# Gap fills of the exponential tables moved to VectorE, 32-bit fills, and tap weights of 52 columns in an S4 + MLP block

## The chip, the core and the metric

One core of a Trainium2 chip runs the whole kernel. The metric is the device time of one execution in microseconds (us). The five engines that matter have their own instruction streams: TensorE (PE, with its weight loads PEld), VectorE (DVE), ScalarE (ACT), GpSimd (POOL) and SyncE (SP, which issues most DMAs). [...] Against the kernel before, a difference of about 0.3% can be told from none.

## What is computed

```python
def _A_ref(u, A_re, A_im, B_re, B_im, C_re, C_im, log_dt, Dskip):
    dt = jnp.exp(log_dt)[:, None]
    logdA = dt * (A_re + 1j * A_im)
    P = jnp.exp(logdA[:, :, None] * l[None, None, :])        # l = 0 .. 2047, in bf16
    K = jnp.einsum("dn,dnl,dn->dl", Cc, P, dt * Bc).real     # the convolution's taps
    ...                                                      # causal convolution of u with K, + u * Dskip

x = A_u                                                      # 1 x 2048 x 512
h = x + _A_ref(_layernorm(x), ...)                           # 512 channels, 128 states each
h2 = h + _B_ref(_layernorm(h), ...)                          # layernorm, MLP 512 -> 1376 -> 512 with gelu
```

## The kernel before

The powers `P` are not tabulated for every `l`. An index is split in two, and a table of each half is kept per channel: the A half has 20 rows (`NA`), the B half has 33 (`NB`). The product of a row of A with a row of B, summed over the 128 states, is one tap, and TensorE makes it by a matrix product whose contraction runs over the states.

**Tables.** `EA` and `EB` hold the real parts, `IA` and `IB` the imaginary parts, in four chunks of 128 channels (`c` = 0 to 3). All lie in one large SBUF tile named `ar`. Inside a chunk four channels are interleaved: the words of one group of four channels are `4*NP_` (A) or `4*NB` (B) values in a row, a table row being four neighbouring values. `NP_` is 32, so that of 32 rows of an A table only 20 are computed; rows 20 to 31 are the gap, and are filled with zeros by `gap` (L756 in the profile). `EA` is filled in two pieces of two chunks each, `IA` chunk by chunk. Before the change each fill writes bf16 values: 64 runs of 48 values for two chunks of `EA`, 32 runs of 48 for one chunk of `IA`. All five are on GpSimd.

**Start.** GpSimd zeroes a scrap that TensorE uses to clear PSUM (L1459, L1466), then builds the identity matrix `identb` (L752, L753). TensorE spreads `log_dt` over the partitions (L710), ScalarE takes the exponential (L701), TensorE transposes the raw parameters with the identity (L809, L840), and VectorE makes the decay rates: `th[1]` is a product from PSUM (L689) and `th[0]` its negative (a `tensor_scalar` of 512 float32 values, L675). From `th` ScalarE makes 16 exponentials for `EB` (L793), while VectorE goes on with the angles (L694, L677, L689), the size of the coefficients (L847, L852) and the layernorm of the first half of the input (L923, L931). Then ScalarE makes the exponentials of `EA` (L991), and the angles go through DRAM (`S_d`, `HL_d`) to be restacked. Sines of the angles (L1026 for B, L1063 for A) are multiplied into the tables by VectorE (L1036, L1043 and L1068).

**Taps.** `kgen(c)` makes the taps of a chunk: for each group `q` of channels (32 groups, by way of `i`), two column tiles of TensorE (`t` = 0 and 1, at column 0 and 64) each get two matrix products, the real one and the imaginary one, that accumulate into the same PSUM words (L1092). The weights are the A table of a pair of channels, read with a step of four values; the moving operand is the pair's B table, 66 columns, also with a step of four. That is 128 products a chunk, 512 in all. Two channels give 2 x 32 = 64 weight columns: 20 rows and 12 of the gap for the first, the same for the second. Then the result is copied out (`evac`, L616 on ScalarE or L618 on VectorE), and later steps read rows 0 to 19 of each 32.

**Order.** Nothing is scheduled at run time. Every step is an operation with a number in the order in which the code adds it, and the list `ORDER` says in which order they are issued: an entry is twice the operation's number, plus one where the second of its possible engines is taken. Each engine does its own in that order. Entries 54 and 56 are the two fills of `EA`.

Of the kernel before, what the change touches and what calls it, by code (L numbers as in the profile page):

```python
# [11 lines left out]
f32 = mybir.dt.float32  # L12
# [8 lines left out]
CW = 128  # L21
# [4 lines left out]
NA = len(ROWS)  # L26
NP_ = 32
NB = 33
# [247 lines left out]
class VS(V):  # L276
# [13 lines left out]
LAG = {"PE": 0.12, "ACT": 0.20, "DVE": 0.14, "POOL": 0.15, "SP": 0.15}  # L290
OWN = {"PE": 0.0, "ACT": 0.17, "DVE": 0.11, "POOL": 0.1, "SP": 0.0}
ORDER = [
# [35 lines left out]
]  # L328
SLOTS = "0124626046204620462406220246200626224606446426424602606426042060242042604206246240264024604620406240245651620426262341302560134076205472541326036260721452042067563414307136506437056253104574107423"

# [110 lines left out]
def kernel(ctx, tc, A_u, A_A_re, A_A_im, A_B_re, A_B_im, A_C_re, A_C_im, A_log_dt, A_Dskip,  # L441
# [220 lines left out]
    def POOL(cost, f, r=(), w=(), pr=None, hv=0):  # L662
        add("POOL", cost, lambda e: f(), r=r, w=w, pr=pr, hv=hv)
# [88 lines left out]
        gp.memset(identb.ap(), 0.0)  # L752
        gp.affine_select(out=identb.ap(), in_=identb.ap(), pattern=[[-1, P]], compare_op=ALU.not_equal, fill=1.0, base=0, channel_multiplier=1)  # L753
    POOL(0.5, ident_fn, w=[identb], pr=0)
    def gap(tabs, pr):
        POOL(0.8 * len(tabs), lambda: gp.memset(free(tabs[0].lo // 2 + 4 * NA, [[4 * NP_, CW // 4 * len(tabs)], [1, 4 * (NP_ - NA)]]), 0.0), w=[t[NA:NP_] for t in tabs], pr=pr)  # L756
    gap(EA[0:2], 0.05)
    gap(EA[2:4], 0.051)

    def split(x, hl, pr, m=1.0):  # L760
        TS(hl[0], x, m, None, ALU.mult, pr=pr)
# [314 lines left out]
    def kgen(c, pr):  # L1076
# [3 lines left out]
        for grp in KIS:  # L1080
            S.pr = pr + 0.01 * KIS.index(grp)
            p = Ps(n=len(grp))
            first = True
            for nb, (i0, n) in enumerate(grp):
                for lo, hi in ((0, n // 2), (n // 2, n)):
                    def fn(e, p=p, nb=nb, i0=i0, lo=lo, hi=hi):
                        for i in range(lo, hi):
                            for t in range(2):
                                q, f = 16 * t + 2 * ((i0 + i) // 4), (i0 + i) % 4
                                o = pst(p)[64 * t:64 * t + 64, 512 * nb + 2 * NB * i:512 * nb + 2 * NB * i + 2 * NB]  # L1090
                                for ta, tb in ((Ar, Br), (Ai, Bi)):
                                    pe.matmul(o, lhsT=free(ta.lo // 2 + q * 4 * NP_ + f, [[4, 2 * NP_]]), rhs=free(tb.lo // 2 + q * 4 * NB + f, [[4, 2 * NB]]), start=ta is Ar, stop=ta is Ai, tile_position=(0, 64 * t))  # L1092
                    add("PE", 0.064 * (hi - lo), fn, r=[Ar, Br, Ai, Bi], w=[p], new=[p] if first else [])
                    first = False
            i0, n = grp[0]
            N = len(grp)

            def ofn(i0=i0, n=n, N=N):
                return ks().rearrange("p z k i -> p (z k) i")[:, :, i0:i0 + n * N].rearrange("p q (b i) -> p q b i", b=N)

            def ifn(p=p, n=n, N=N):
                return pst(p).rearrange("p (b q) -> p b q", b=N)[:, :, 0:2 * NB * n].rearrange("p b (i q) -> p q b i", q=2 * NB)
            evac(ofn, ifn, 2 * NB * n * N, [p], [kg])
# [397 lines left out]
```

## Time and profile before

| | |
|---|---|
| median of three runs | 233.96 us (233.57 to 234.28) |
| the profiled execution | 234.25 us, of it 232.5 us span of the core |
| granted TensorE clock | 0.989 |
| GpSimd busy | 21.7 us (9%), 28 instructions |
| fills by L756 | 2 of 128x3072 bf16, 3 of 128x1536 bf16 |
| tap products, L1092 | 512, matmul rows 18.5 us and weight load rows 17.3 us in all |

Rows of the profile name a line of the kernel and an engine. A row's duration runs from the start of an instruction to its end, so that it includes any time in which the engine held the instruction and could not go on. Matmul rows overlap: the pace of a sequence is its length over its count, not the mean of a row. "Idle before, releaser" is what the engine waited for. PE share says little, as matmuls are pipelined.

### The profile page before, as it was taken

The numbers are of one execution on the slowest core, as the hardware profiler recorded it, in microseconds if no ns is written. First come the engines' busy times: TensorE is split into PE (matmuls) and PEld (weight loads), VectorE is DVE, ScalarE is ACT, GpSimd is POOL, SyncE is SP. The second block draws the span as 40 slices with busy tenths as digits, with TensorE's granted clock in tenths as the row PEclk, the third lists the DMA queues.
The fourth block names the chain that finished last, engine by engine and source line by source line (L and its number), as shares of the span: only waits on it lengthen the run. The fifth ranks groups of instructions, "written<-read, shape, count | busy, mean of one in ns | idle before, by whom it ended". The sixth has DMA issues, their size and how long they took to land.

```text
span 232.5 us, 6866 instructions
## 1 busy us (share of the span) xinstructions
PE 198.0 (85%) x2981; PEld 114.3 (49%) x2981; DVE 173.0 (74%) x277; ACT 164.3 (71%) x203; POOL 21.7 (9%) x28
## 2 busy tenths in 40 slices
PE   7205579576999999999999878999999999999993
PEld 4002453233775569756567465554444434444452
DVE  2999968999797997688899979989965557113022
ACT  4699999999898997998997687685325404903700
POOL 8200030500020000300000030110000101000000
PEclk9999999999999999999999979999999999999998
DMA  5960173135004956585897991009831052051202
GB/s 157 208 107 17 48 182 93 48 102 181 3 6 93 182 154 162 154 174 146 194 226 161 252 266 40 3 0 226 93 71 42 3 126 68 11 121 40 68 17 73
DMA packets 43159, 25.09 MB, mean 108 GB/s; under 512 B 30197, under 2 KB 40697, under 8 KB 43130
## 3 DMA queue, kind: packets, MB, share of 16 engines
q1 hardware_dynamic: 41576, 22.72, 43.2%
q10 hardware_dynamic: 1554, 1.93, 2.7%
q8 instruction: 23, 0.38, 0.7%
q14 instruction: 6, 0.05, 0.1%
HBM read 14.13 MB, written 5.28 MB: 83 GB/s over the span
## 4 chain that ended last, share of the span: by engine, by line
PE 43%; DVE 30%; ACT 15%; issue 5%; DMA 4%; POOL 1%; ACTq 0%; SPq 0%; DVEq 0%; POOLq 0%
PE ps L1378 13%; PE ps L1362 11%; PE ps L1092 7%; ACT ar L616 6%; ACT ar L1063 5%; DVE ar L1235 5%; DVE ar L689 5%; DVE ar L1210 4%; ACT ar L991 3%; DVE ar L694 3%; PE ps L1245 2%; DVE ar L1323 2%; DVE ar L923 2%; DMA HL_d<-ar 2%; PE ps L946 2%
## 5 line engine op out<-in xcount | busy, mean ns | idle before, releaser
L616 ACT CAST ar<-ps 128x1024 bf16<-128x1024 f32 (+3 forms) x73 | 62.5, 917 | 11.3 <-PE ps L1245 5.7
L1364 ACT ACTIVATE ar<-ps,ar 128x512 bf16<-128x512 f32 (+1 forms) x44 | 27.4, 684 | 34.1 <-PE ps L1362 28.6
L1362 PE MATMUL ps<-ar 128*128 128x512 bf16 (+1 forms) x176 | 40.1, 379 | 0.1
L1378 PE MATMUL ps<-ar 128*128 128x512 bf16 (+3 forms) x187 | 40.2, 367 | 0.0
L1380 DVE TENSOR_TENSOR ar<-ps,ar 128x512 bf16<-128x512 f32 (+1 forms) x17 | 10.6, 654 | 26.7 <-issue 19.7
L1378 PEld LDWEIGHTS <-ar 128*128 128x128 bf16 (+1 forms) x187 | 17.8, 97 | 19.7 <-issue 0.7
L1362 PEld LDWEIGHTS <-ar 128*128 128x128 bf16 (+1 forms) x176 | 17.3, 100 | 20.2 <-issue 0.5
L1235 DVE TENSOR_TENSOR ar<-ar 128x2048 bf16<-128x2048 bf16 x20 | 24.0, 1219 | 1.3 <-PE ps L1245 0.9
L618 DVE CAST ar<-ps 128x1024 bf16<-128x1024 f32 (+4 forms) x18 | 19.5, 1092 | 7.3 <-PE ps L1092 2.6
L1245 PE MATMUL ps<-ar 64*128 64x128 bf16 x672 | 23.2, 225 | 1.9 <-DVE ar L1235 1.7
L1245 PEld LDWEIGHTS <-ar 64*128 64x128 bf16 x672 | 20.4, 99 | 6.9 <-DVE ar L1235 4.1
L689 POOL TENSOR_TENSOR ar<-ar 128x4 f32<-128x4 f32 (+1 forms) x6 | 9.5, 1577 | 140.9 <-DVE ar L694 101.8
L1063 ACT ACTIVATE ar<-ps 128x1024 bf16<-128x1024 int16 x20 | 19.5, 1038 | 1.7 <-PE ps L1061 1.5
L1092 PE MATMUL ps<-ar 128*64 128x66 bf16 x512 | 18.5, 243 | 0.4 <-issue 0.4
L1092 PEld LDWEIGHTS <-ar 128*64 128x64 bf16 x512 | 17.3, 147 | 2.8 <-issue 2.5
L793 ACT ACTIVATE ar<-ar 128x1024 bf16<-128x1024 f32 x16 | 15.6, 1042 | 2.7 <-DVE ar L675 2.7
L946 PE MATMUL ps<-ar 128*32 128x512 bf16 x256 | 16.4, 381 | 1.0 <-DVE ar L931 0.9
L1026 ACT ACTIVATE ar<-ps 128x1024 bf16<-128x1024 int16 x16 | 15.8, 1037 | 0.4 <-PE ps L1018 0.4
L1061 PE MATMUL ps<-ar 128*32 128x256 f16 (+1 forms) x256 | 12.9, 300 | 3.0 <-ACT ar L1063 2.8
L967 PE MATMUL ps<-ar 128*64 128x128 bf16 (+2 forms) x160 | 13.7, 298 | 0.9 <-ACT ar L616 0.9
L694 DVE SCALAR_TENSOR_TENSOR ar<-ar 128x4 f32<-128x4 f32 (+3 forms) x33 | 9.9, 305 | 5.9 <-POOL ar L689 5.4
L1068 DVE TENSOR_TENSOR ar<-ar 128x1024 bf16<-128x1024 bf16 x20 | 13.0, 684 | 0.6 <-ACT ar L1063 0.4
(82 smaller groups left out, 234.4 us busy)
## 6 DMA issues: line engine op xcount, KB each, us to landing
ar<-in_A_u_dram SPq DMA_DIRECT2D x16, 128.0 KB
ar<-in_A_u_dram SPq DMA_DIRECT2D x8, 256.0 KB
out_dram<-ar SPq DMA_DIRECT2D x30, 64.0 KB
ar<-in_B_w_dram SPq DMA_DIRECT2D x3, 344.0 KB
AK_d<-ar SPq DMA_DIRECT2D x2, 512.0 KB
AKc_d<-ar SPq DMA_DIRECT2D x4, 256.0 KB
ar<-tab_TP SPq DMA_DIRECT2D x1, 768.0 KB
ar<-AKc_d SPq DMA_DIRECT2D x3, 256.0 KB
```

Source lines behind the costliest of these rows:

```text
L616: act.copy(out_fn(), in_fn())
L618: dve.tensor_copy(out_fn(), in_fn())
L689: add(eng, tuple(c[q] for q in eng), lambda e: (dve if e == "DVE" else gp).tensor_tensor(oap() if oap else o.ap(), aap() if aap else a.ap( ...
L694: add("DVE", c_dve(n, 1, psum), lambda e: dve.scalar_tensor_tensor(oap() if oap else o.ap(), aap() if aap else a.ap(), f(s), bap() if bap ...
L946: pe.matmul(pst(p)[32 * j:32 * j + 32, 512 * z:512 * z + 512], lhsT=BX.ap()[:, f0 + z, 16 - 16 * c:48 - 16 * c], rhs=src[2 * j + c].ap(), ...
L1063: add("ACT", c_act(1024), lambda e, sc=sc: act.activation(sc.ap().rearrange("p z a b -> p (z a b)").rearrange("p (x a f) -> p a x f", a=4, ...
L1092: pe.matmul(o, lhsT=free(ta.lo // 2 + q * 4 * NP_ + f, [[4, 2 * NP_]]), rhs=free(tb.lo // 2 + q * 4 * NB + f, [[4, 2 * NB]]), start=ta is ...
L1235: dve.tensor_tensor(pq.ap().rearrange("p n d -> p (n d)"), a, b_, ALU.mult)
L1245: pe.matmul(pst(p)[:, 512 * h + 128 * k:512 * h + 128 * k + 128], lhsT=q.ap()[rows, x, :], rhs=TP[w].ap()[rows, f0 // 2 + k, :], start=(n ...
L1362: pe.matmul(pst(p)[:fs], lhsT=w1s[dc].ap()[:, fc * P:fc * P + fs], rhs=ybuf.ap().rearrange("p (t c) k -> p c t k", c=4)[:, dc], start=(dc ...
L1364: add("ACT", c_act(512, 1), lambda e, p=p, fc=fc, fs=fs: act.activation(hT.ap()[:fs, fc, :], pst(p)[:fs], ACT.Gelu_apprx_tanh, bias=b1_sb. ...
L1378: pe.matmul(pst(p)[:, c0:c1], lhsT=hT.ap()[:fs, fc, 128 * t:128 * t + 128], rhs=w2s[fc].ap()[:fs, c0:c1], start=(fc == 0), stop=(fc == NFC ...
```

## The change

The two fills of `EA` go to VectorE, ahead of its first product; the three of `IA` stay with GpSimd. All five write float32 words, half as many as bf16 values before. The tap products take 52 columns of weights (32 + 20): the second channel's 12 gap columns are left off, and PSUM partitions 52 to 63 (and 116 to 127) aren't written any more; nothing reads what they would hold.

```diff
 ORDER = [
-    2, 0, 52, 4, 58, 50, 62, 154, 6, 64, ...
+    2, 0, 52, 4, 58, 54, 56, 50, 62, 154, 6, 64, ...
...
-    def gap(tabs, pr):
-        POOL(0.8 * len(tabs), lambda: gp.memset(free(tabs[0].lo // 2 + 4 * NA, [[4 * NP_, CW // 4 * len(tabs)], [1, 4 * (NP_ - NA)]]), 0.0), w=[t[NA:NP_] for t in tabs], pr=pr)
-    gap(EA[0:2], 0.05)
-    gap(EA[2:4], 0.051)
+    def gap(tabs, pr, eng="POOL"):
+        add(eng, 0.8 * len(tabs), lambda e: (gp if eng == "POOL" else dve).memset(V(ar, tabs[0].lo, f32, (CW // 4 * len(tabs), 2 * NP_)).ap()[:, :, 2 * NA:], 0.0), w=[t[NA:NP_] for t in tabs], pr=pr)
+    gap(EA[0:2], 0, "DVE")
+    gap(EA[2:4], 0, "DVE")
...
-                                o = pst(p)[64 * t:64 * t + 64, 512 * nb + 2 * NB * i:512 * nb + 2 * NB * i + 2 * NB]
+                                o = pst(p)[64 * t:64 * t + 32 + NA, 512 * nb + 2 * NB * i:512 * nb + 2 * NB * i + 2 * NB]
                                 for ta, tb in ((Ar, Br), (Ai, Bi)):
-                                    pe.matmul(o, lhsT=free(ta.lo // 2 + q * 4 * NP_ + f, [[4, 2 * NP_]]), rhs=free(tb.lo // 2 + q * 4 * NB + f, [[4, 2 * NB]]), start=ta is Ar, stop=ta is Ai, tile_position=(0, 64 * t))
+                                    pe.matmul(o, lhsT=free(ta.lo // 2 + q * 4 * NP_ + f, [[4, NP_ + NA]]), rhs=free(tb.lo // 2 + q * 4 * NB + f, [[4, 2 * NB]]), start=ta is Ar, stop=ta is Ai, tile_position=(0, 64 * t))
```

VectorE's stream at its beginning, as a piece of the difference (`ar` is the SBUF tile, `ps` PSUM; L708 writes the row of ones for L710, L788 a small constant):

```order
 L708 MEMSET ar 1x128
 L788 MEMSET ar 128x1
+L756 MEMSET ar 128x64x24 x2
 L689 TENSOR_TENSOR ar<-ps,ar 128x512 [waits PE_49,Activation_49]
 L675 TENSOR_SCALAR ar<-ar 128x512 [waits DVE_49]
```

Two fills of 64 runs of 24 words now stand ahead of L689, the first product, and ahead of its wait for TensorE and ScalarE.

GpSimd's stream at the same place and as far as the first fills of `IA` (L901 is a small constant, L1394 and L1395 set the middle row of the B tables):

```order
 L753 AFFINE_SELECT ar<-ar 128x128 [waits Pool_49]
 L901 MEMSET ar 128x16
-L756 MEMSET ar 128x64x48 x2
 L1394 MEMSET ar 128x32x4 x2
 L689 TENSOR_TENSOR ar<-ar 128x8 [waits DVE_49,Pool_49]
 L1394 MEMSET ar 128x32x4
 L1395 MEMSET ar 128x32x4 [waits DVE_49,Activation_49]
-L756 MEMSET ar 128x32x48
+L756 MEMSET ar 128x32x24
```

The two fills of 64 runs of 48 values are gone from GpSimd, and its small fills L1394 follow right behind L901. The fills of `IA` keep their places with half the values in a run. TensorE, ScalarE and SyncE issue the same instructions in the same order as before, the tap products with 52 weight columns for 64.

70 rows, old and new, of the table ORDER are left out of this document.

## The prediction

> **What bounds the kernel now.** I read the chain of waits first, for the stages that set the end, then in time order for its first 12 us, where the fills are.
>
> ```profile
> PE 43%; DVE 30%; ACT 15%; issue 5%; DMA 4%; POOL 1%; ACTq 0%; SPq 0%; DVEq 0%; POOLq 0%
> PE ps L1378 13%; PE ps L1362 11%; PE ps L1092 7%; ACT ar L616 6%; ACT ar L1063 5%; DVE ar L1235 5%; DVE ar L689 5%; DVE ar L1210 4%; ACT ar L991 3%; DVE ar L694 3%; PE ps L1245 2%; DVE ar L1323 2%; DVE ar L923 2%; DMA HL_d<-ar 2%; PE ps L946 2%
> ```
>
> The bound moves from engine to engine. The fills L756 do not appear in it; the tap products L1092 do, with 7%.
>
> ```profile
> 3.71 0.61 PE ps L809 x4
> 4.42 0.70 DVE ar L689
> 5.15 2.52 DVE ar L675
> 7.67 0.60 DVE ar L694
> ```
>
> From 4.42 us VectorE is the chain. One piece is out of proportion: L675, a `tensor_scalar` of 512 float32 values, for 2.52 us. The views of single lines (shortest, median, longest in ns) and the timeline say why.
>
> ```profile
> L675 DVE TENSOR_SCALAR ar<-ar x6: 420/428/2524, 5.1 to 40.8; 128x512 f16<-128x512 f32 x5, 128x512 f32<-128x512 f32 x1
> L677 DVE TENSOR_SCALAR ar<-ar x4: 420/426/427, 8.3 to 39.6; 128x512 f32<-128x512 f32 x4
> L1394 POOL MEMSET ar<- x4: 199/204/205, 7.0 to 69.5; 128x128 bf16 x4
> 1.84 5.26 POOL L756 MEMSET ar<- 128x3072 bf16 x2
> 7.04 0.35 POOL L1394 MEMSET ar<- 128x128 bf16 x2
> 7.71 2.00 ACT L793 ACTIVATE ar<-ar 128x1024 bf16<-128x1024 f32 x2 [2.70 <-DVE ar L675]
> ```
>
> The same form (L677) takes 0.43 us. Taking that from the end of L675 (5.15 + 2.52 = 7.67) gives 7.24 us; GpSimd's two fills end at 1.84 + 5.26 = 7.10, and the first L1394 at 7.04 + 0.20 = 7.24. So L675 stood until GpSimd paused, 2.52 - 0.43 = **2.1 us**, and ScalarE's L793 stood behind it. L689, from 4.42 to 5.12 in the middle of the same fills, took its usual 0.70: not every VectorE form is stopped, but this one is.
>
> Is there room behind the stall? A table by stage (columns: stretch, then busy us of PE, PEld, DVE, ACT, POOL, then clock, DMA share, GB/s):
>
> ```profile
> 8.00:16.00 8.00, 0.00 (x0) 0.10 (x1) 7.83 (x14) 8.00 (x9) 0.00 (x0) 1.00 0.88 169
> 16.00:26.00 10.00, 3.17 (x37) 1.67 (x40) 9.86 (x18) 10.00 (x13) 0.00 (x0) 1.00 0.07 24
> 26.00:37.00 11.00, 9.09 (x209) 6.43 (x202) 7.76 (x22) 10.98 (x13) 2.11 (x2) 1.00 0.67 164
> ```
>
> From 8 to 26 us VectorE and ScalarE are both full, to 37 us ScalarE still is. Both start behind L675, so both move as a whole.
>
> **The change part by part: the stall.** GpSimd's two fills leave; after the identity (L753, rows below, to 1.85) it has L901 and two L1394 of 0.20 left, and is done by about 2.4 us, long before L675 comes. The stall goes: **-2.1 us** where L675 ends. What is late next? Loads that do not move. The layernorm's first reading (L923) stands at 19.95 us, and would stand at 17.85; PE's first use of the table of identity weights (L865) at 17.55, and would at 15.45:
>
> ```profile
> 13.68 0.10 PEld L865 LDWEIGHTS <-ar 128*32 128x32 f16 x1 [6.87 <-DMA ar<-tab_I]
> 17.55 0.37 PE L865 MATMUL ps<-ar 128*32 128x256 f16 x1 [10.44 <-DVE ar L675]
> 19.95 0.68 DVE L923 BATCH_NORM_STATS2 ar<-ar 128x6 f32<-128x512 bf16 x1
> 14.00:16.00 2.00, 0.00 (x0) 0.00 (x0) 1.97 (x3) 2.00 (x3) 0.00 (x0) 1.00 0.27 40
> ```
>
> That table has landed at 13.68, and DMA falls to 0.27 between 14 and 16 us, so the input is in by then; about 2 us are left over. SP issues the `S_d` and `HL_d` transfers when VectorE has made their contents, so they come 2.1 us earlier too, and the tables behind them in SP's queue with them. I see nothing with a fixed time that eats the gain; I keep 1.9 to 2.2.
>
> **The fills on VectorE.** Two instructions of 64 x 24 = 1536 words, between L788 and L689. No such fill is in the trace; the nearest are VectorE's own small ones.
>
> ```profile
> L788 DVE MEMSET ar<- x1: 59/59/59, 0.9 to 0.9; 128x1 f32 x1
> L1280 DVE MEMSET ar<- x1: 112/112/112, 8.2 to 8.2; 128x64 uint32 x1
> 0.72 0.62 POOL L1459 MEMSET ar<- 1x640 bf16 x1 [0.29 <-POOLq L1485]
> 0.81 0.17 DVE L708 MEMSET ar<- 1x128 bf16 x1 [0.81 <-PEq L1485]
> 0.92 0.06 DVE L788 MEMSET ar<- 128x1 f32 x1
> 1.29 0.20 POOL L752 MEMSET ar<- 128x128 bf16 x1
> 1.56 0.29 POOL L753 TENSOR_SCALAR_AFFINE_SELECT ar<-ar 128x128 bf16<-128x128 bf16 x1
> ```
>
> 63 more words cost 53 ns, 0.84 ns each: 1536 words take 1.35 us, two 2.7 us. From 0.98 they end at 3.7, and L689 cannot start before L809 ends at 3.71 + 0.61 = 4.32. The cover is 4.42 - 0.98 = 3.4 us, so I cost them at **0**. As an upper bound for a word I take L689's own rate, 0.70 us for 512 values, 1.37 ns: 2.1 us each, end 5.2, L689 0.8 late. If the cover goes (a shorter PSUM clearing, say), they cost their 2.7.
>
> [...]
>
> Beside them GpSimd builds the identity (L752, L753, 1.29 to 1.85), which L809 needs at 3.7: a fill that kept GpSimd out of SBUF until 3.7 would make L809 0.6 late (0.20 + 0.29 and hand-over). Before, L708 and L788 ran inside GpSimd's L1459, and L708's 128 values took 0.17, no more per value than L1280's 64 in 0.11, so I take 0.
>
> **The `IA` fills** on GpSimd get shorter or stay (half the values). Nobody waits for L756 by its own view, and GpSimd is 9% busy: 0 either way. Should L1394 or these ever meet a `tensor_scalar`, each costs at most its length.
>
> **52 columns.** Nearly all of L1092 is on the path: its pieces in the chain, of which the first, the two longest and the last are shown, add up to 497 of the 512, one half in each of two stages (to 71 us, and from 83.6 us). What sets their pace?
>
> ```profile
> 59.17 2.37 PE ps L1092 x68
> 68.61 2.41 PE ps L1092 x68
> 87.32 4.21 PE ps L1092 x130
> 94.65 1.15 PE ps L1092 x32
> ...
> 87.16 4.38 PE L1092 MATMUL ps<-ar 128*64 128x66 bf16 x132
> 107.86 0.64 PE L967 MATMUL ps<-ar 128*64 128x128 bf16 x16
> L1092 PE MATMUL ps<-ar 128*64 128x66 bf16 x512 | 18.5, 243 | 0.4 <-issue 0.4
> L967 PE MATMUL ps<-ar 128*64 128x128 bf16 x64 | 2.5, 221 | 0.0
> L1092 PEld LDWEIGHTS <-ar 128*64 128x64 bf16 x512 | 17.3, 147 | 2.8 <-issue 2.5
> L967 PEld LDWEIGHTS <-ar 128*64 128x64 bf16 x160 | 7.0, 110 | 5.0 <-issue 3.3
> L1362 PEld LDWEIGHTS <-ar 128*96 128x96 bf16 x16 | 2.0, 122 | 1.7 <-issue 0.3
> L946 PEld LDWEIGHTS <-ar 128*32 128x32 bf16 x256 | 5.9, 96 | 7.6 <-issue 2.3 <-DVE ar L931 1.2
> ```
>
> The pace is (4.38 - 0.24) / 131 = 31.6 ns for L1092, and (0.64 - 0.22) / 15 = 28.0 ns for L967, which also alternates two column tiles of 64 weight columns, but reads 128 moving columns without a step. L1092's 66 columns take as long a row as L967's 128 (243 for 221), and its weight load of 64 columns is 37 ns longer than L967's. So both of its operands, read with a step of four, seem to come at about half rate: 66 like 132. Were the moving side alone the limit, the pace would be 28.0 x 132 / 128 = 28.9 ns; it is 31.6, so I read the weight load as the limit, by 2.7 ns. A column of weights costs (122 - 96) / 64 = 0.41 ns, at half rate 0.81: 12 fewer save 9.8 ns a load, 4.9 with two tiles side by side, more than the 2.7. Then the moving side limits: 2.7 ns x 497 = **-1.3 us**. Bounds: 0 if the load does not limit; 31.6 x 12 / 64 = 5.9 ns x 512 = 3.0 us if the load is all there is. I stay at 1.3, the one that a row (L967) prices. ScalarE and VectorE have to follow:
>
> ```profile
> 58.50:72.00 13.50, 13.09 (x368) 10.29 (x356) 12.19 (x16) 11.73 (x14) 1.52 (x2) 1.00 0.02 4
> 83.50:97.00 13.50, 13.46 (x360) 11.66 (x360) 9.88 (x24) 11.46 (x15) 2.16 (x2) 1.00 0.49 134
> ```
>
> In both stages PE is full and they have 1.3 to 3.6 us to spare, so 0.65 each fits.
>
> **Sum.** 234.25 (the profiled execution: 232.5 span and 1.75 around it) - 2.1 - 1.3 = 230.85. That execution lay 0.29 above the median of 233.96, so against it: **230.6 us**.
>
> **The rivals.** *Only the stall goes.* The moving 66 columns set L1092's pace and the 31.6 is theirs, with some loss from the step; narrower weights change no pace. For it: matmul rows are stretched (243) just as the loads are. Against: L967's 28.0. 234.25 - 2.1, on the median's scale 231.9.
> [...]
>
> *Only the taps gain.* The wait of L675 reappears: the fills on VectorE end late, or VectorE and GpSimd block each other at 1 to 4 us, or L675 waits for something other than GpSimd. Against: the end at 7.24 to the hundredth. 234.25 - 1.3, so 232.7.
>
> *Neither*: 234.0, no change.
>
> *Slower: the fill pays for each run.* VectorE's fill has 64 runs of 24 words; if each costs a start like L788's 59 ns, a fill takes 1.35 + 64 x 0.059 = 5.1 us, two end at 11.2, L689 is 6.8 late, and the whole chain behind it: 234.25 + 6.8 - 2.1 - 1.3, so 237.4. A fill starts to cost over 1.72 us (half of 3.44), and over 3.4 us both gains are gone. Against: GpSimd's fills have the same 64 runs, and 3072 values in 2.66 us (half of 5.26 and a hand-over) are no dearer per value than 128 in 0.20.
>
> **How the numbers follow.** Both gains 0.60 (its own range 229.2 to 231.5: start 1.9 to 2.2, taps 0.5 to 2.8); only the stall 0.20; only the taps 0.10; neither 0.05; slower 0.05. The predicted time is the first case's, 230.6. The range 229.2 to 232.8 takes in the first three and leaves out the last two and the tails. Faster by over 0.3% (under 233.26; about what a measurement of this kernel can tell) are the first three, 0.90; within 0.3% 0.05; slower 0.05.
>
> **What would show it.** Right: L675 near 5.15 us takes 0.43, L793 starts near 5.6, L756 on VectorE twice about 1.35 us and over before 4.3, HL_d and everything to 48 us 2.1 earlier, L1092 at 28 to 29 ns. Wrong: L689 after 4.5 us (the fills are too long), L675 long again, L923 or L865 with a DMA for releaser (a load is next), L1092 still at 31 to 32 ns, or ScalarE idle no less between 58 and 72 us.

## The result, and the profile after

| | before | after |
|---|---|---|
| median of five runs each | 233.96 us (233.37 to 234.34) | 230.90 us (230.66 to 231.47) |
| the profiled execution | 234.25 us, span 232.5 | 230.71 us, span 228.9 |
| granted TensorE clock in it | 0.989 | 0.997 |
| L675, longest | 2.52 us | 0.43 us |
| pace of L1092 | 31.6 ns | 31.2 ns |

The ratio is 0.9876, with a 95% interval of 0.9851 to 0.9900: faster by 2.3 to 3.5 us.

The page of the changed kernel, its chain by engine and by line:

```profile
PE 53%; ACT 26%; DVE 10%; DMA 4%; issue 4%; POOL 1%; ACTq 0%; SPq 0%; DVEq 0%; POOLq 0%
PE ps L1362 17%; PE ps L1378 17%; ACT ar L616 8%; PE ps L1092 7%; ACT ar L793 7%; ACT ar L1063 5%; ACT ar L991 4%; PE ps L1245 4%; DVE ar L1235 2%; DMA HL_d<-ar 2%; PE ps L946 2%; DMA ar<-AKc_d 2%; DVE ar L971 1%; DVE ar L1068 1%; ACT ar L701 1%
```

VectorE's share fell from 30% to 10% and ScalarE's rose from 15% to 26%. That is a change of route more than of work: between 8 and 26 us both engines are full (VectorE 17.8 of 18 us, ScalarE 18.0), and the chain now goes back over ScalarE's L793 where it went over VectorE's L694 and L689. L1092 keeps its 7%.

The timeline of the start (start, duration, engine, line, what; in brackets the idle time before and its releaser):

```profile
1.25 1.34 DVE L756 MEMSET ar<- 128x1536 f32 x1 [0.27 <-issue]
1.84 0.35 POOL L1394 MEMSET ar<- 128x128 bf16 x2
2.86 1.34 DVE L756 MEMSET ar<- 128x1536 f32 x1 [0.27 <-issue]
4.42 0.69 DVE L689 TENSOR_TENSOR ar<-ps,ar 128x512 f32<-128x512 f32 x1 [0.22 <-ACT ar L701]
5.15 0.43 DVE L675 TENSOR_SCALAR ar<-ar 128x512 f32<-128x512 f32 x1
5.61 2.00 ACT L793 ACTIVATE ar<-ar 128x1024 bf16<-128x1024 f32 x2 [0.60 <-DVE ar L675]
...
15.45 0.37 PE L865 MATMUL ps<-ar 128*32 128x256 f16 x1 [8.69 <-DVE ar L675]
...
17.84 0.68 DVE L923 BATCH_NORM_STATS2 ar<-ar 128x6 f32<-128x512 bf16 x1
```

L675 takes its usual 0.43 us at the same start of 5.15, and L793 starts at 5.61 where it started at 7.71. The loads behind do not eat the gain: L865 and L923 come 2.1 us earlier, at 15.45 and 17.84, and L865 still waits for VectorE, not for a DMA. The fills end at 2.86 + 1.34 = 4.20, 0.22 ahead of L689. But a row of 1.34 reads short: the two starts lie 1.61 us apart, and the 0.27 of "idle" before each belongs to the fill. 1.61 us for 1536 words are 1.05 ns a word.

The groups of the tap products (count, then busy us and mean ns of a row), one long run of them, and the second of their two stages (busy us of PE, PEld, DVE, ACT, POOL, then clock, DMA share, GB/s):

```profile
L1092 PE MATMUL ps<-ar 128*52 128x66 bf16 x512 | 18.3, 242 | 0.4 <-DVE ar L1068 0.4
L1092 PEld LDWEIGHTS <-ar 128*52 128x52 bf16 x512 | 16.8, 128 | 2.7 <-issue 1.8 <-DVE ar L1068 0.6
```

```profile
84.94 4.33 PE L1092 MATMUL ps<-ar 128*52 128x66 bf16 x132
```

```profile
81.00:94.00 13.00, 13.00 (x348) 11.00 (x344) 9.74 (x22) 11.32 (x15) 2.16 (x2) 1.00 0.45 128
```

The weight load became 19 ns shorter (147 to 128), the matmul row 1 ns (243 to 242), and the pace is (4.33 - 0.24) / 131 = 31.2 ns. PE is as full in its stage as before (13.00 of 13.00 us, and 13.46 of 13.50 before). The copies out of PSUM (L616 and L618, 128x924 values in their rows) still read all 128 partitions, those that are no longer written included; only the steps behind them leave these rows out.

**Where the two profiled executions part.** The start of the same instruction in both, from the views of the chain and the timeline:

| instruction | before | after | earlier by |
|---|---|---|---|
| L793, first | 7.71 | 5.61 | 2.10 |
| L1092, first | 59.17 | 57.07 | 2.10 |
| L616, after the last tap products | 96.83 | 94.53 | 2.30 |
| L971, its run of four | 114.96 | 112.27 | 2.69 |
| L1380, the last of VectorE | 228.93 | 225.39 | 3.54 |

So 2.1 us come from the start, 0.2 from the tap stages, 0.4 at L971, which nobody had foreseen, and 0.85 later. The last is put down to TensorE's clock and not to the change. The stretch from 132 to 141 us, before the change and then after it, and the same 64 products in both (they start 2.70 us apart, and what follows them 3.4 to 3.7):

```profile
132.00:141.00 9.00, 5.67 (x106) 4.42 (x100) 7.22 (x16) 7.32 (x11) 1.93 (x1) 0.81 0.99 249
...
135.58 3.41 PE L1245 MATMUL ps<-ar 64*128 64x128 bf16 x64 [1.68 <-DVE ar L1235]
```

```profile
132.00:141.00 9.00, 7.00 (x154) 5.45 (x155) 8.09 (x13) 7.82 (x14) 1.69 (x1) 1.00 0.84 171
...
132.88 1.96 PE L1245 MATMUL ps<-ar 64*128 64x128 bf16 x64 [1.46 <-DVE ar L1235]
```

TensorE was granted 0.81 of its clock there on average in the profiled execution of before (0.50 from 136 to 138 us), and the full clock in that of after. Why such a dip comes is not shown; it comes in some executions of nearly every kernel here. Of the 23 executions of before beside the first experiments, the four at a granted clock of 1.0 took 233.0 to 233.3 us, those at 0.985 to 0.990 took 234.0 to 234.5, about 1 us more. The mean clock alone doesn't tell what a dip costs: the two executions at 0.948 and 0.956 took 233.1 and 233.3.

The two executions of after at 1.0 took 230.7 and 230.9. Without dips the difference is so some 2.1 to 2.7 us; the three terms 2.1, 0.2 and 0.4 add up to 2.7, its upper end.

### The profile page after: what moved, and what is told of

Its sections match the earlier page's. It is cut to its first block, busy times and chain, and to the rows that moved or that the text cites. A ratio compares the mean times of both kernels' runs of the same rounds, so it can differ in the third digit from the quotient of the medians.

```text
span 228.9 us, 6859 instructions
## 1 busy us (share of the span) xinstructions
PE 196.2 (86%) x2974; PEld 113.6 (50%) x2981; DVE 173.5 (76%) x279; ACT 164.4 (72%) x203; POOL 14.6 (6%) x26
## 4 chain that ended last, share of the span: by engine, by line
PE 53%; ACT 26%; DVE 10%; DMA 4%; issue 4%; POOL 1%; ACTq 0%; SPq 0%; DVEq 0%; POOLq 0%
PE ps L1362 17%; PE ps L1378 17%; ACT ar L616 8%; PE ps L1092 7%; ACT ar L793 7%; ACT ar L1063 5%; ACT ar L991 4%; PE ps L1245 4%; DVE ar L1235 2%; DMA HL_d<-ar 2%; PE ps L946 2%; DMA ar<-AKc_d 2%; DVE ar L971 1%; DVE ar L1068 1%; ACT ar L701 1%
## 5 line engine op out<-in xcount | busy, mean ns | idle before, releaser
L616 ACT CAST ar<-ps 128x1024 bf16<-128x1024 f32 (+3 forms) x73 | 62.4, 917 | 10.8 <-PE ps L1245 5.3
L1380 DVE TENSOR_TENSOR ar<-ps,ar 128x512 bf16<-128x512 f32 (+1 forms) x17 | 10.6, 652 | 26.7 <-issue 19.7
L618 DVE CAST ar<-ps 128x1024 bf16<-128x1024 f32 (+4 forms) x18 | 19.5, 1091 | 6.6 <-PE ps L1092 2.5
L1245 PE MATMUL ps<-ar 64*128 64x128 bf16 x672 | 21.5, 216 | 1.9 <-DVE ar L1235 1.5
L1245 PEld LDWEIGHTS <-ar 64*128 64x128 bf16 x672 | 19.1, 94 | 6.5 <-issue 3.2
L1092 PE MATMUL ps<-ar 128*52 128x66 bf16 x512 | 18.3, 242 | 0.4 <-DVE ar L1068 0.4
L689 POOL TENSOR_TENSOR ar<-ar 128x4 f32<-128x4 f32 (+1 forms) x6 | 9.5, 1577 | 143.3 <-DVE ar L694 104.6
L1092 PEld LDWEIGHTS <-ar 128*52 128x52 bf16 x512 | 16.8, 128 | 2.7 <-issue 1.8
L793 ACT ACTIVATE ar<-ar 128x1024 bf16<-128x1024 f32 x16 | 15.6, 1044 | 0.6 <-DVE ar L675 0.6
L694 DVE SCALAR_TENSOR_TENSOR ar<-ar 128x4 f32<-128x4 f32 (+3 forms) x33 | 9.9, 305 | 6.4 <-POOL ar L689 5.4
L967 PE MATMUL ps<-ar 128*64 128x128 bf16 (+2 forms) x160 | 13.6, 298 | 0.9 <-ACT ar L616 0.9
(83 smaller groups left out, 229.0 us busy)
```

What stands on the lines that cost most here:

```text
L616: act.copy(out_fn(), in_fn())
L618: dve.tensor_copy(out_fn(), in_fn())
L793: add("ACT", c_act(1024) + 0.03, lambda e, e0=e0: act.activation(free(EB0 // 2 + 4 * (16 - e0), [[8 * e0, 2], [4 * NB, NCH * CW // 4], [1, ...
L1092: pe.matmul(o, lhsT=free(ta.lo // 2 + q * 4 * NP_ + f, [[4, NP_ + NA]]), rhs=free(tb.lo // 2 + q * 4 * NB + f, [[4, 2 * NB]]), start=ta is ...
L1245: pe.matmul(pst(p)[:, 512 * h + 128 * k:512 * h + 128 * k + 128], lhsT=q.ap()[rows, x, :], rhs=TP[w].ap()[rows, f0 // 2 + k, :], start=(n ...
```

## The experiments

The questions: which part of the change removes the stall, what sets the pace of the taps, how near the fills are to the path, and what happened at L971. Medians of before beside them lay between 233.68 and 233.95 us. "Before" or "after" behind a label is the kernel that the edit starts from.

**The fills alone** (e1, after).

```diff
-o = pst(p)[64 * t:64 * t + 32 + NA, ...]
+o = pst(p)[64 * t:64 * t + 64, ...]
-lhsT=free(ta.lo // 2 + q * 4 * NP_ + f, [[4, NP_ + NA]])
+lhsT=free(ta.lo // 2 + q * 4 * NP_ + f, [[4, 2 * NP_]])
```

> The change without its narrow weights (64 columns again). Theory: the fills give the 2.1 us of L675's stall, and the 52 columns next to nothing, since the changed kernel's tap products still go at 31.2 ns (31.6 before). Then this is within 0.3 us of the changed kernel: 231.0 to 231.3, L1092 back at 31.6 ns. Rival (the 52 columns give the 1.3 us forecast for them): 232.2.

231.55 us (230.75 to 231.84), ratio 0.9899 [0.9878, 0.9920]. The start is that of after row by row, and the long run of tap products takes 0.02 us more than with 52 columns:

```profile
85.11 4.35 PE L1092 MATMUL ps<-ar 128*64 128x66 bf16 x132
```

(4.35 - 0.24) / 131 = 31.4 ns. L971's run of four starts at 112.49, 0.22 later than in after (112.27): that is all that the taps brought. The median is 0.25 above what was expected. Most of the 0.65 us between it and that of after is likely dips: five of these six executions had one, and the sixth, at a clock of 1.0, took 230.75.

**The narrow taps alone** (e2, before, with the two lines of e1 the other way round).

> The 52 columns alone, fills as before. Theory: 0.1 to 0.3 us faster than before, 233.7; L675 keeps 2.52 us, L1092 at 31.2 ns, its weight load rows shorter (128 ns for 147), its matmul rows unchanged. Rival (the weight load sets the pace somewhere): 1 us or more, 232.7 or less.

233.73 us (232.79 to 234.37), ratio 0.9997 [0.9980, 1.0014], over twelve executions. The stall stands as before, and the pace is (4.33 - 0.24) / 131 = 31.2:

```profile
5.15 2.52 DVE L675 TENSOR_SCALAR ar<-ar 128x512 f32<-128x512 f32 x1
...
87.06 4.33 PE L1092 MATMUL ps<-ar 128*52 128x66 bf16 x132
```

The weight load shrank here too, from 147 to 129 ns a row, and the interval takes in no change. The weight load did not set the pace; the forecast's 1.3 us is not there.

**32-bit fills on GpSimd** (e3, before). Fills not moved, 64 columns.

```diff
-gp.memset(free(tabs[0].lo // 2 + 4 * NA, [[4 * NP_, CW // 4 * len(tabs)], [1, 4 * (NP_ - NA)]]), 0.0)
+gp.memset(V(ar, tabs[0].lo, f32, (CW // 4 * len(tabs), 2 * NP_)).ap()[:, :, 2 * NA:], 0.0)
```

> The kernel before with 32-bit fills and nothing else: the fills stay on GpSimd, at their old place, with 64 columns. Theory (what counts is that GpSimd is done when L675 comes at 5.15 us, not who fills): the GpSimd fills halve to about 1.4 us each and end by 4.7 us, L675 takes 0.43 us, the time is that of the fills-only run, 231.0 to 231.3. Rival (GpSimd must not fill at all beside VectorE's work, or L675 waits for something else): L675 stays over 1 us, 232.5 to 234.

```profile
1.84 2.70 POOL L756 MEMSET ar<- 128x1536 f32 x2
4.42 0.69 DVE L689 TENSOR_TENSOR ar<-ps,ar 128x512 f32<-128x512 f32 x1 [3.44 <-ACT ar L701]
4.48 0.35 POOL L1394 MEMSET ar<- 128x128 bf16 x2
5.15 0.43 DVE L675 TENSOR_SCALAR ar<-ar 128x512 f32<-128x512 f32 x1
```

GpSimd's fill, too, costs by values and not by bytes here: half the values in as many bytes take 2.70 us for 5.26. Its fills end at 4.54, before L675 comes, and the stall is gone without a fill being moved. The time, 231.97 us (231.31 to 232.10), ratio 0.9913 [0.9892, 0.9934], is 0.7 above what was expected: 0.4 of it is L971 (below), the rest dips in four of six executions (the two at a clock of 1.0 took 231.3).

**16-bit fills on VectorE** (e4, after). The pieces of EA are filled as bf16 values, with ones. The IA fills on GpSimd are bf16 again too (1.38 us each in before, 0.74 in after; by the views of L756 nobody waits for them there).

```diff
-.memset(V(ar, tabs[0].lo, f32, (CW // 4 * len(tabs), 2 * NP_)).ap()[:, :, 2 * NA:], 0.0)
+.memset(free(tabs[0].lo // 2 + 4 * NA, [[4 * NP_, CW // 4 * len(tabs)], [1, 4 * (NP_ - NA)]]), 0.0 if eng == "POOL" else 1.0)
```

> The changed kernel with the two fills on VectorE in bf16, 3072 values each for 1536 words (filled with ones, which nothing reads). The fill's true price is told by what it delays. Theory (one value takes 1.04 ns, as the 1.61 us from one fill's start to the next's shows, and the row of 1.34 us leaves 0.27 out): 3.2 us each, the second ends at 7.4, L689 3.0 us late, 233.9. Rival (the rows are right, 0.84 ns a value): the second ends near 6.2, L689 1.8 late, 232.7. Rival (a start is paid for each of the 64 runs): later than 10 us, 237 or more.

```profile
1.57 2.62 DVE L756 MEMSET ar<- 128x3072 bf16 x1 [0.59 <-issue]
4.78 2.62 DVE L756 MEMSET ar<- 128x3072 bf16 x1 [0.59 <-PE ps L809]
7.33 0.62 DVE L689 TENSOR_TENSOR ar<-ps,ar 128x512 f32<-128x512 f32 x1
7.98 0.43 DVE L675 TENSOR_SCALAR ar<-ar 128x512 f32<-128x512 f32 x1
```

From start to start 4.78 - 1.57 = 3.21 us for 3072 values, 1.04 ns each, the same as for a word of 32 bits. L689 comes 2.9 us later than in after, and the median is 233.91 us (233.58 to 234.75), ratio 1.0009 [0.9993, 1.0024]: to move the fills without halving them would have brought nothing.

**The operands of the taps without their step** (e5 and e6, after; one execution each). Other values are multiplied, so the taps are others.

```diff
-rhs=free(tb.lo // 2 + q * 4 * NB + f, [[4, 2 * NB]])
+rhs=free(tb.lo // 2 + q * 4 * NB + f, [[1, 2 * NB]])
```

> The changed kernel; the moving operand of the tap products is 66 neighbouring values, not every fourth (the taps come out as other numbers, the work is the same). Theory (the moving operand, read at half rate because of its step, sets the 31.2 ns): the matmul rows fall from 242 by some 28 ns to about 215, and the pace below 27 ns. Rival (two products in a row on one column tile, or the weight load, set it): pace still 30 to 32 ns.

```profile
L1092 PE MATMUL ps<-ar 128*52 128x66 bf16 x512 | 15.2, 216 | 0.4 <-DVE ar L1068 0.4
L1092 PEld LDWEIGHTS <-ar 128*52 128x52 bf16 x512 | 14.4, 145 | 2.8 <-issue 1.8 <-DVE ar L1068 0.6
...
83.16 3.48 PE L1092 MATMUL ps<-ar 128*52 128x66 bf16 x132
```

(3.48 - 0.22) / 131 = 24.9 ns, 6.3 below after; 228.69 us. L971 comes 2.85 us earlier than in after. The 24.9 need not be the moving operand's own pace: L967 passes 128 columns without a step in 28.0 ns, by which 66 would take some 14 (an estimate: 28.0 x 66 / 128). So something else may limit here, and the step itself may cost more than 6.3.

```diff
-lhsT=free(ta.lo // 2 + q * 4 * NP_ + f, [[4, NP_ + NA]])
+lhsT=free(ta.lo // 2 + q * 4 * NP_ + f, [[1, NP_ + NA]])
```

> The changed kernel; the weights of the tap products are 52 neighbouring values, not every fourth (other taps, same work). Theory (the moving operand sets the pace): the weight load rows fall from 128 to about 105 ns, the pace stays at 31 ns. Rival (the weight load still sets it): pace 28 ns or less.

```profile
L1092 PEld LDWEIGHTS <-ar 128*52 128x52 bf16 x512 | 16.3, 121 | 2.5 <-issue 1.6 <-ACT ar L616 0.4 <-DVE ar L1068 0.2
...
84.39 4.25 PE L1092 MATMUL ps<-ar 128*52 128x66 bf16 x132
```

(4.25 - 0.24) / 131 = 30.6 ns, 0.6 below after, and 230.63 us. The weight load rows fell to 121 ns only, not to the 105 that was expected. Taking the step from the moving operand brings 6.3 ns a product, taking it from the weights a tenth of this: the moving 66 columns, read with their step, set the pace.

**The two tiles in turn** (e7, after; e8 the same with 64 columns, one execution).

```diff
-for t in range(2):
-    ...
-    for ta, tb in ((Ar, Br), (Ai, Bi)):
+for ta, tb in ((Ar, Br), (Ai, Bi)):
+    for t in range(2):
```

> The changed kernel with the two column tiles taking turns: real product of tile 0, real of tile 1, imaginary of 0, imaginary of 1, for 0, 0, 1, 1. The 28.9 ns of the forecast came from L967, which takes turns. Theory (two products in a row on one tile leave a gap, since the second one's operands wait for the first): pace 28 to 29.5 ns, tap stages 0.5 us shorter each, 229.7 to 230.4. Rival (each product's own moving read, 66 columns at half rate, sets the pace in any order): pace 31 ns, 230.9.

> As the run before, with 64 weight columns again. Theory: if taking turns brings the pace under 30 ns, the weight load is the next limit and 64 columns cost something again, a pace 1 to 2.5 ns above that of 52 columns. Rival: the same pace as with 52 columns, so the width plays no part in either order.

A run of 132 takes 4.33 us in e7, as in after, and in e8 4.35, as in e1. e7 took 231.46 us (230.67 to 231.62), ratio 0.9890 [0.9867, 0.9913], e8 230.90. The order of the tiles brings nothing with either width, as the rivals said.

**A short clearing of PSUM, and the fills late** (e9, e10 and e11, after). e9 makes only one of the four products L1466 that clear PSUM with zeros; e10 also returns the fills of EA to GpSimd, as words, at about 40 us; e11 returns them with all four products.

```diff
-zero(zs[:4])
+zero(zs[:1])
```

> The changed kernel with one of the four PSUM-clearing matmuls (L1466) at the start, so that L710, the exponential and L809 can come up to 1.1 us earlier; the fills stay on VectorE ahead of L689. It takes away the cover of the fills. Theory (a fill holds VectorE 1.61 us, the second to 4.2 us, whatever its row of 1.34 says): L689 starts near 4.2, not 3.3; 230.7. Rival (the fills are done by 3.6, as row lengths from 0.98 would say): L689 near 3.6, 230.1. Rival (the parameters come too late, or TensorE is slower without the clearing): L689 at 4.4, 230.9 or more.

```profile
2.86 1.34 DVE L756 MEMSET ar<- 128x1536 f32 x1 [0.27 <-issue]
3.14 1.16 PE L809 MATMUL ps<-ar 128*128 128x128 bf16 x8 [0.19 <-DMA ar<-in_A_A_re_dram]
4.13 0.61 DVE L689 TENSOR_TENSOR ar<-ps,ar 128x512 f32<-128x512 f32 x1
4.78 0.43 DVE L675 TENSOR_SCALAR ar<-ar 128x512 f32<-128x512 f32 x1
```

230.42 us (230.24 to 231.32), ratio 0.9853 [0.9831, 0.9874]. TensorE's L809 comes 0.5 us earlier and now waits for a load; L675 comes 0.37 earlier, and L689 stands behind the second fill without a gap: now the fills come last.

```diff
-2, 0, 52, 4, 58, 54, 56, 50, 62, ...
+2, 0, 52, 4, 58, 50, 62, ...
...
-348, 280, 492, ...
+348, 280, 54, 56, 492, ...
...
-gap(EA[0:2], 0, "DVE")
-gap(EA[2:4], 0, "DVE")
+gap(EA[0:2], 0)
+gap(EA[2:4], 0)
```

> The same short clearing, with the two EA fills as 32-bit words on GpSimd right behind the IA fills, at 40 us and over. Nothing is then left on VectorE ahead of L689. Theory: L689 near 3.3 us, L675 takes 0.43 there, and all of the 1.1 us is kept: 229.8, faster than the changed kernel by 1 us. Rival (the next limit at the start, ScalarE's table load or the loads, comes within 0.3 us): 230.6. Rival (fills at 40 us stand in the way of VectorE's or TensorE's work there): slower than 230.9.

```profile
2.94 1.21 PE L809 MATMUL ps<-ar 128*128 128x128 bf16 x8 [0.29 <-DMA ar<-in_A_A_re_dram]
3.72 0.69 DVE L689 TENSOR_TENSOR ar<-ps,ar 128x512 f32<-128x512 f32 x1 [2.74 <-PE ps L809]
4.45 0.43 DVE L675 TENSOR_SCALAR ar<-ar 128x512 f32<-128x512 f32 x1
```

Without the fills L689 comes at 3.72, 0.70 earlier than in after and 4.13 - 3.72 = 0.4 earlier than in e9. About half of this is not the fills: L809 waits for its parameters in both traces, and they came 0.2 us later in e9 (3.14 for 2.94). In e10 as in after L689 starts 0.78 us behind the start of L809, which in e9 would be 3.92; so the fills cost some 0.2 us there, 0.4 at most, and not their 2.7. What L675 gains over e9, 0.33 us, is given back at L971 (below): 230.48 us (230.40 to 231.02), ratio 0.9865 [0.9845, 0.9885], no better than e9. The 229.8 of the theory is missed by 0.7: L689 comes at 3.72 and not near 3.3, and 0.37 goes at L971.

> The changed kernel with full clearing and only the EA fills moved, to GpSimd at 40 us, as 32-bit words. Theory (on VectorE they stand inside its 3.4 us of waiting and cost nothing, at 40 us GpSimd's fills stop nobody): the time of the changed kernel, 230.7 to 231.2, L689 at 4.42. Rival (the fills on VectorE cost something that L689's start does not show): 0.5 us faster.

With the full clearing and the fills away L689 and L675 start at 4.43 and 5.15, as in after: the fills on VectorE cost nothing there. But the time is 231.96 us (231.83 to 232.09), ratio 0.9922 [0.9904, 0.9939], 1 us above after. That missed what was expected by 0.8, and no row of the start answers for it. 0.4 stands at L971, and its six executions all had a dip (clock 0.993 or less); that the dips are the rest is not shown.

**Two small instructions more on VectorE** (e12, e3 with L788 three times instead of once). In before and e2, e3, e10 and e11 L971 starts 0.36 to 0.37 us later behind L967 than in after and e1, e4 to e9. The second set has two VectorE instructions more ahead of it, the fills; so the theory is that L971's place in VectorE's stream counts, and the rival that GpSimd's fills do.

```diff
-lambda e: dve.memset(tiny.ap(), 1e-36)
+lambda e: [dve.memset(tiny.ap(), 1e-36) for _ in range(3)]
```

> The kernel before with 32-bit fills on GpSimd (the run e3), and the one-value fill L788 on VectorE three times for once. Its two more instructions do no work, but VectorE's stream is as long again ahead of L689 as in the changed kernel. It is about the 0.37 us by which a VectorE instruction (L971, near 112 us) starts later after its wait in every kernel whose EA fills are on GpSimd, and in none where VectorE has them. Theory (it is the place in VectorE's instruction stream at which that wait falls, and two instructions more move it): in the profile L971 starts about 0.07 us after its wait's row, as in the changed kernel, and the time is 0.3 to 0.4 us under that of e3: 231.6. Rival (GpSimd's fills themselves do it): 0.42 us after the wait's row, 232.0.

231.39 us (231.03 to 231.84), ratio 0.9900 [0.9878, 0.9922], beside e3's 231.97; at a clock of 1.0 it is 231.0 beside 231.3. The same run of four in before, after, e3, e11 and e12, in this order:

```profile
114.96 2.48 DVE L971 TENSOR_TENSOR ar<-ps,ar 128x512 bf16<-128x512 f32 x4 [0.76 <-PE ps L967]
```

```profile
112.27 2.48 DVE L971 TENSOR_TENSOR ar<-ps,ar 128x512 bf16<-128x512 f32 x4 [0.39 <-PE ps L967]
```

```profile
112.81 2.48 DVE L971 TENSOR_TENSOR ar<-ps,ar 128x512 bf16<-128x512 f32 x4 [0.75 <-PE ps L967]
```

```profile
112.70 2.48 DVE L971 TENSOR_TENSOR ar<-ps,ar 128x512 bf16<-128x512 f32 x4 [0.75 <-PE ps L967]
```

```profile
112.58 2.48 DVE L971 TENSOR_TENSOR ar<-ps,ar 128x512 bf16<-128x512 f32 x4 [0.39 <-PE ps L967]
```

With a constant written twice more, 110 us earlier, the wait falls from 0.75 to 0.39, GpSimd's fills being those of e3. In all fourteen kernels, by one trace of each, it is 0.75 or 0.76 without the two instructions and 0.39 with them. The place in the stream counts; why it does no run here shows.

## Why the prediction was near, and where it was wrong

Forecast 230.6 us, measured 230.9, in the range and with the sign. But the sum was 2.1 + 1.3, and what was found is 2.1 + 0.2 + 0.4 and a share of dips that fell on one side. That the total came so near is partly luck: 1.1 us too much for the taps was made up by 0.4 at L971 and by the dips.

**The stall: right, to the hundredth.** L675 at 5.15 for 0.43, L793 at 5.61, L865 at 15.45 and L923 at 17.84 stand where they were put, and everything to the tap stages is 2.1 us earlier. The cause holds as well: e3 leaves the fills on GpSimd and only lets them end at 4.54, ahead of L675, and the stall is gone. No semaphore explains the stall: L675's only wait, in the stream shown with the change, is for VectorE itself (DVE_49). What held it instead no run shows. What is shown is that L675 stood for 2.1 us while GpSimd filled, and takes 0.43 us when GpSimd's fills are over (e3) or not there (after); L689, a product of 512 values with one operand from PSUM, had its 0.69 us in the middle of the same fills.

**The fills at nothing: right, with less cover than the rows gave.** The row has 1.34 us where 1.35 was put, and the end at 4.20 was asked to be before 4.3. But a fill really takes 1.61 us, of which its row leaves out 0.27. From 0.98 two of them end at 4.20, where the second row ends too, and not at the 3.7 of the prediction; before L689 at 4.42 that leaves 0.22 us of cover and not 4.42 - 3.7 = 0.7. e4 shows how narrow it was: at 3.21 us a fill the whole gain is gone. The rival that each run of 24 words costs a start is refuted: it put a fill at 5.1 us, and 1.61 us are 1.05 ns a word.

**"If the cover goes, they cost their 2.7": wrong.** e9 and e10 put the cost at 0.2 us, 0.4 at most, since the loads that L809 waits for come next and cover the rest.

**52 columns, -1.3 us: the mis-sized term.** The step that failed is "I read the weight load as the limit, by 2.7 ns". The load rows shrank by 19 ns, 147 to 128, about twice the 9.8 that was put, and still the pace only went from 31.6 to 31.2 ns; over 497 products that is 0.2 us, and e2 alone shows no difference. The rival *Only the stall goes* had the mechanism: e5 takes the step from the moving operand, and the pace falls to 24.9. What misled is the floor of 28.9 ns, an estimate, L967's 28.0 scaled to 132 half-rate columns; 66 columns with a step took 31.2 ns, and 30.6 in e6. That 66 stepped columns pass like 132 of L967's is not so: they take 2.3 ns longer than that, and why stays open. For the weights half rate isn't borne out either: without the step their load rows fell by 7 ns, 128 to 121 (e6). In e7 the tiles take turns after each product, and it brings nothing (4.33 us for 132 products in either order), so it isn't that two products follow each other in a tile.

**The sign and the total.** By mechanism the second case (231.9) came nearer than the first. It lacks what L971 gave, 0.4 us, and the dips: the predicted scale was a median of before with dips in it, and two of five executions of after had one. With 0.2 for the taps instead of 1.3 the forecast would have been 231.7, 0.8 too slow. The lower end of the first case's own range, 229.2, is counted from 234.25 and the upper from 233.96; from the median both ways it would be 229.0.

**What it said would show it.** L1092 at 28 to 29 ns is the sign that failed; "still at 31 to 32" had been named as what would make it wrong. ScalarE's idle time hardly fell: 13.50 - 11.73 = 1.8 us in the first tap stage of before, 13.10 - 11.47 = 1.6 in the same stage after, from the row below.

```profile
56.40:69.50 13.10, 12.74 (x360) 9.83 (x357) 11.89 (x16) 11.47 (x14) 0.89 (x2) 1.00 0.02 4
```

**A better version.** e9, the change with the short clearing, has the lowest median of the kernels that compute the block, 230.42 us; its interval (0.9831 to 0.9874) overlaps that of after, so that it is the better one is likely and not shown. The medians favour it: four of its five executions ran at a clock of 1.0 (230.2 to 230.4 us), and two of after's (230.7 and 230.9). The 0.4 us between these are seen in the traces at L675, 4.78 for 5.15.

## What to carry to other kernels

A `tensor_scalar` of float32 values that takes several times its usual length beside a long GpSimd instruction (here 2.52 us for 0.43) may be a stall that the profile counts as busy time, and the cheapest cure here was to make the GpSimd instruction shorter: a fill cost per value, so that words of 32 bits halved it, on either engine (two fills 5.26 to 2.70 us on GpSimd, one 3.21 to 1.61 on VectorE). Before a matmul's weights are narrowed, ask which operand sets the pace, and test it by taking the step from one operand at a time; here the moving one had the step that cost, 6.3 ns of 31.2 against 0.6 for the weights' step. Price a fill by the distance between starts, and hold a saving of some tenths of a microsecond against kernels that differ only in the number of instructions, since that alone moved L971 by 0.37 us here.

## What was not expected of the hardware

- A VectorE fill's row is shorter than the fill: 1.34 us for 1.61 (1536 words) and 2.62 for 3.21 (3072 bf16 values). The rest stands as idle time before it, in rows that name "issue" or, in e4, TensorE as the releaser.
- A wait for TensorE ended 0.37 us earlier or later by two instructions more or less on VectorE, 110 us before it: 0.39 in nine kernels, 0.75 or 0.76 in five.
- A step of four bf16 values in the moving operand lengthened the pace of 66 columns from 24.9 to 31.2 ns.
- About 1 us of the difference between two executions of the same kernel goes with TensorE's granted clock: before took 233.0 to 233.3 us at 1.0 and 234.0 to 234.5 at 0.985 to 0.990. In the profiled one it was 0.50 from 136 to 138 us, and 64 products took 3.41 us for 1.96.
